# First expert job drawn from 13 tiles with its transposes behind the last logits; value sums in thirds; keys' first sums over all partitions

## The chip, the cores and the metric

The kernel runs on one NeuronCore of a Trainium2 chip. The metric is the device time of one execution in microseconds (us), the median of several runs; lower is better. The engines are TensorE (PE; its weight loads are listed as PEld), VectorE (DVE), ScalarE (ACT), GpSimd (POOL) and SyncE (SP, which here only issues DMAs). Each engine works through its own list of instructions in order; semaphores hold an instruction until what it reads is there and what it overwrites has been read. The lists are made ahead of time by a scheduler that moves instructions among each other by its own estimates; only dependencies and a few hand-written constraints bind it.

## The reference

Four batches of 8 heads with 576 positions of 64 values go through an attention that adds two parts: a full softmax attention over sums of four neighbouring positions, repeated four times, and a local one over positions less than 4 apart. The result, 2304 tokens of 512, goes through two mixture-of-experts layers, each with 8 experts.

```python
q_d = q.reshape(B, H, Sd, 4, D).mean(axis=3)           # k_d, v_d alike
out_up = np.repeat(sm_attn(q_d, k_d, v_d), 4, axis=2)
...
mask = np.abs(pos[:, None] - pos[None, :]) < 4
...
attn_out = out_up + np.matmul(attn, v)
x = attn_out.transpose(0, 2, 1, 3).reshape(B * S, H * D)
...
e_idx = np.argmax(x @ w_gate, axis=1)                   # one expert for each token
for e in range(8):
    h = np.maximum(x[e_idx == e] @ w1[e], 0.0)          # 512 -> 1024
    out[e_idx == e] = gate * (h @ w2[e])                # 1024 -> 512
```

The first layer has a second gate on its output. With these inputs the first layer sends 404 of the 2304 tokens to expert 0, the most, and 361 to expert 3. Of the first 14 tiles (1616 tokens) expert 0 has 253 and expert 3 has 244; of the first 13 tiles (1500 tokens) they have 242 and 236.

## The kernel before

**Attention.** `attention()` walks over 20 tiles (`NTP` = 5 for each batch) of up to 116 tokens in a software pipeline: in step `s` tile `s` has its local scores (`Local.scores`, L606) and softmax, tile `s-1` its transposes and products (L663), and tile `s-2` is turned (`xflip`, L683, `xtevac`, L687) and multiplied with the gate weights (`lmm`, L377, then `lsel`, L702, and a copy to `lgs`, L705). The pooled attention of a batch (`Pooled`) runs in the steps of the batch before; batch 0's runs ahead of the loop, in an order written by hand (`PRO`).

**The pooled sums.** `sums_k` adds four keys at a time into `kpd`, `sums_q` queries into `qd`, `sums_v` values into `vpd`. DVE does batch 0 (keys and queries with a reduction, L465) and POOL nearly all else (two additions: a first level into `tm`, L467, a second from it, L468; for the values L471 within `vraw`, then L474). Keys of the two heads of a pair lie in the lower and upper 64 partitions and go to different places of `kpd`, so `sums_k` runs once for each half of the partitions.

**Routing.** Tiles are routed in groups (`GROUPS`, first tile and count). When a group's last tile has its logits, `pick` finds each token's expert, `count` (matmuls L286 to L293 into `pos`) numbers the tokens within each expert, `place` (L309 to L337) computes each token's place and adds the group's totals to `base` (L311), and for each tile `spread` (L344 to L350: `am`, `oc`, `bm`) and `put` (a matmul into the PSUM tile `list`, L357) write token number and gate into the expert's list. `lT` (logits) and `pos` share one PSUM buffer, `ps_misc`. From step `PUTS` on two puts are issued in a step.

**The first expert job.** At the end of step `SNAP` `early()` runs: `snap` takes the expert that has the most tokens in the groups that are placed by then, `fetch` reads its first 256 entries from the list (`li`, L1039; `ri`, L1161) and POOL gathers those rows of `x0` (two indirect DMAs, L1144). `seen` tells which rows of `x0` that gather can touch. If the expert has fewer than 256 tokens so far, the rest of the job is empty rows, and its later tokens start at place 256. `prime` starts the loads of the first three weight tiles (`raw`). Behind attention `xpose` turns the gathered rows (L1194), ACT makes `xh` (L1198) and DVE the remainder `xl` (L1201); `split_next` does the same to weights (`wh`, L1115; `wl`, L1123). The first `wh` is held behind tile 19's L687 by a hand-written constraint.

**The jobs.** A product is three matmuls (`mm3`, L1276 to L1278). Job 0 is 192 such matmuls of 256 columns, `ph` then `py`, and the last groups' puts stand among them. Job 1 takes the same expert's remaining tokens from the finished lists and reuses its weights; a loop for experts whose lists overflow their job (`overflow`, L1284) follows, with no passes if every list fits. Seven more jobs with fixed sizes (`CAPS`) follow, and then the second layer.

Of the kernel before, what the change touches and what calls it, by code (L numbers as in the profile page):

```python
# [9 lines left out]
F32 = mybir.dt.float32  # L10
# [4 lines left out]
ALU = mybir.AluOpType  # L15
# [5 lines left out]
B, H, S, D = 4, 8, 576, 64  # L21
NP = H // 2
SD = S // 4
# [19 lines left out]
)  # L43

HEAD = (256, 256)
GROUPS = ((0, 5), (5, 4), (9, 5), (14, 4), (18, 2))
SNAP = 18
NWE = 3
POOLSPLIT = 0
POOLHI = 0  # L50
REM0 = 0
PUTN = 2
PB = (3, 2, 3, 2, 1)
PUTS = 15
PRI = 100
LOH = 1
NWARM = 3
# [123 lines left out]
def moe_pair_kernel(  # L181
# [17 lines left out]
    nc = tc.nc  # L199
# [164 lines left out]
    def route_all(*a, fast=0, **kw):  # L364
# [6 lines left out]
        for t in range(T):  # L371
            spread(t, fast)
            put(t)

    def logits(m, xT, n, lT, after=None):
        for g in range(4):
            i = nc.tensor.matmul(  # L377
                lT[32 * g:32 * g + 32, 0:n], lhsT=wgs[m][:, g, :], rhs=xT[:, g, 0:n],
                tile_position=(0, 32 * g), start=True, stop=True, skip_group_check=True,
            )  # L380
            if after is not None:
                tc.add_manual_dep(
                    i.ins, after.ins.name,
                    mybir.DependencyInfo(mybir.DependencyClass.Sync, mybir.DependencyReason.DATA),
                    reason="the four column tiles run side by side",
                )


    def attention(actx, early, early_x, front):
# [3 lines left out]
        sb2 = actx.enter_context(tc.tile_pool(name="a_sb2", bufs=2, side="right"))  # L393
# [5 lines left out]
        kd, qt = kq  # L399
        vd = [side[i].tile([128, NG, NP, D], F32, name=f"vd{i}") for i in range(2)]  # L400
        kpd = [side[i].tile([128, 2, NP, SD], F32, name=f"kpd{i}") for i in range(2)]
        vraw = sbe.tile([128, 3, 4, NP, 65], F32, name="vraw")
        vpd = [side[i].tile([128, 3, 2, NP, 65], F32, name=f"vpd{i}") for i in range(2)]
# [38 lines left out]
        def sums_k(b, c, n, eng=None):  # L442
            eng = eng or nc.vector
            a = slice(c, c + n)
            tm = tmp() if eng is nc.gpsimd else None
            for s in range(2):
                o = slice(64 * s, 64 * s + 64)
                src = kd[b % 3][o, a, 3:3 + S].rearrange("p a (t r) -> p a t r", r=4)
                pool4(eng, kpd[b % 2][o, s, a], src, tm[o, 0:n] if tm else None)

        def sums_q(b, c, n, eng=None):
            eng = eng or nc.vector
# [7 lines left out]
        def tmp():  # L460
            return sbe.tile([128, 2, SD, 2], F32, tag="tm", name="tm", bufs=2)

        def pool4(eng, dst, src, tm):
            if tm is None:
                eng.tensor_reduce(dst, src, axis=AX.X, op=ALU.add)  # L465
                return
            eng.tensor_tensor(tm, src[:, :, :, 0:2], src[:, :, :, 2:4], op=ALU.add)  # L467
            eng.tensor_tensor(dst, tm[:, :, :, 0], tm[:, :, :, 1], op=ALU.add)  # L468

        def sums_v(b, eng=nc.gpsimd):  # L470
            eng.tensor_tensor(vraw[:, :, 0:2], vraw[:, :, 0:2], vraw[:, :, 2:4], op=ALU.add)  # L471
            for s in range(2):
                o = 64 * s
                eng.tensor_tensor(  # L474
                    vpd[b % 2][o:o + 64, :, s], vraw[o:o + 64, :, 0], vraw[o:o + 64, :, 1], op=ALU.add
                )

        def sums(b, eng_q=None):
            for c in (0, 2):
# [230 lines left out]
        for b in range(B):  # L710
            s0 = NTP * (b - 1) + 2
            for c in range(NP + 1):
                if b or c == NP:
                    pooled_at.setdefault(s0 + c // 2 if b else REM0, []).append(Pooled(b, c))
        groups = GROUPS
        lgs_of = {}
# [29 lines left out]
        for i in range(3):  # L746
            t = sb3.tile([128, 3, 128], F32, tag="p", name="p")
# [58 lines left out]
        for s in range(-1, NL + 3):  # L806
# [6 lines left out]
            if 0 <= s:  # L813
                b, r = s // NTP + 1, s % NTP
# [9 lines left out]
            def ready1():  # L824
                for _ in range(PUTN if s > PUTS else 1):
                    if ready:
                        ready.pop(0)()

            def puts1():
                for _ in range(PUTN if s > PUTS else 1):  # L830
                    if puts:
# [78 lines left out]
            if 6 <= s < 12:  # L910
                o = 384 * (s - 6)
                tc.keep_in_program_order(
                    nc.sync.dma_start(x1[o:o + 384].rearrange("(k p) d -> p k d", p=128), bc1(zx, 3))
                )
            if s > SNAP:
                early_x(s)
            if s == SNAP:
                assert not (puts or defer)
# [39 lines left out]
    def experts():  # L958
# [195 lines left out]
        def fetch(job, fresh=None):  # L1154
# [7 lines left out]
            else:  # L1162
                nc.gpsimd.tensor_copy(ri[:, 0:ns], M.li[:, bass.ds(off, ns), :])
            tiles = max(g + n for g, n in GROUPS if g + n + 2 <= SNAP)
            seen = tiles // NTP * S + tiles % NTP * 2 * GQ
# [19 lines left out]
        def xpose(job, k):  # L1185
            if k == 0:
                xp = pl[f"x{job.i % 2}"]
                job.xT = tuple(xp.tile([128, 4, 512], F32R, tag=t, name=t) for t in ("xh", "xl"))
            xh, xl = job.xT
            mm = job.slots[k][1]  # L1190
            xr = job.x[k]
            pt = psx.tile([128, 4, 128], F32, tag="m", name="t")
            for d in range(4):
                nc.tensor.transpose(  # L1194
                    pt[:, d, 0:mm], xr[0:mm, 128 * d:128 * d + 128], ident[0:mm, 0:mm]
                )
            o = slice(128 * k, 128 * k + mm)
            i = nc.scalar.copy(xh[:, :, o], pt[:, :, 0:mm])  # L1198
            if job.i == 0:
                after.append(i)  # L1200
            nc.vector.tensor_tensor(xl[:, :, o], pt[:, :, 0:mm], xh[:, :, o].bitcast(F32), op=ALU.subtract)  # L1201
# [414 lines left out]
```

## Time and profile before

| | |
|---|---|
| median of 3 runs | 759.45 us (757.87 to 759.95) |
| the profiled execution's own time | 755.45 us |
| its span, first to last instruction | 753.7 us |
| PE busy | 700.1 us, 93% |
| DVE, ACT, POOL busy | 460.0, 342.4, 173.5 us |
| mean granted clock of PE | 0.967 of full speed |

All times below come from the profiled execution, counted from the start of its span. A matmul's busy time is modelled and the matmuls overlap, so a stretch that is fully busy is not a stretch at PE's peak. An instruction that is held inside its engine (not by a semaphore) is shown with a longer duration. The granted clock has two levels, 1.00 for 2.4 GHz and 0.50 for 1.2 GHz.

### The profile page before, as it was taken

The page shows a single profiled execution, that of the slowest core. Times are in us where ns is not written, and L with a number is a line of the kernel's source. Part 1 is how long each engine was busy: PE and PEld are TensorE (multiplying, and loading weights), DVE is VectorE, ACT ScalarE, POOL GpSimd, SP SyncE. Part 2 cuts the span into 40 slices and gives each one's busy share as a digit, 9 for nine tenths or more (in the row PEclk, how much of TensorE's full clock was granted, in tenths as well). Part 3 has the DMA queues.
Part 4 walks back from the last instruction along what each step waited for, and adds up shares of the span by engine and source line. Part 5 has one row for each costly group of instructions (what it writes and reads, how often), then busy time and mean ns, then how long its engine had stood idle before and what let it go on. Part 6 is the DMA issues. An engine that isn't in the chain of part 4 may idle for free. (4 is left out here: it accounts for less than half of the span.)

```text
span 753.7 us, 15825 instructions
## 1 busy us (share of the span) xinstructions
PE 700.1 (93%) x6048; PEld 642.4 (85%) x6048; DVE 460.0 (61%) x1169; ACT 342.4 (45%) x630; POOL 173.5 (23%) x202
## 2 busy tenths in 40 slices
PE   6788699995989999999999999989999999999993
PEld 4557477874979999999999999978999999999992
DVE  8787968786847656565757777535434444455520
ACT  2244366574444435345454463235425353554530
POOL 5774800001031203031211120152013030311111
PEclk9899989996999999999999999989999999999997
DMA  9935635135167535364555452256443544655500
GB/s 359 407 117 205 213 116 186 49 119 169 34 217 220 166 120 171 128 201 134 164 193 167 165 179 97 93 187 214 137 137 130 158 159 155 196 173 192 161 21 16
DMA packets 52990, 120.99 MB, mean 161 GB/s; under 512 B 4800, under 2 KB 26176, under 8 KB 51884
## 3 DMA queue, kind: packets, MB, share of 16 engines
q1 hardware_dynamic: 45772, 99.19, 39.6%
q0 software_dynamic: 7136, 20.72, 8.0%
q8 instruction: 50, 0.82, 0.4%
q14 instruction: 32, 0.26, 0.1%
HBM read 101.01 MB, written 20.71 MB: 162 GB/s over the span
## 5 line engine op out<-in xcount | busy, mean ns | idle before, releaser
L1123 DVE TENSOR_TENSOR wl<-raw,wh 128x1024 fp32r<-128x1024 f32 x128 | 156.2, 1224 | 111.2 <-ACT wh L1115 111.1
L1115 ACT CAST wh<-raw 128x1024 fp32r<-128x1024 f32 x128 | 133.1, 1048 | 199.1 <-PE py L1277 114.3
L1277 PE MATMUL ph<-xl,wh 128*128 128x256 f32 (+8 forms) x576 | 178.1, 311 | 0.2 <-DVE xl L1201 0.2
L1276 PE MATMUL ph<-xh,wh 128*128 128x256 f32 (+8 forms) x576 | 175.0, 312 | 2.6 <-DVE xl L1201 1.9
L1278 PE MATMUL ph<-xh,wl 128*128 128x256 f32 (+8 forms) x576 | 177.2, 309 | 0.0
L1276 PE MATMUL py<-h,wh 128*128 128x256 f32 (+8 forms) x448 | 138.5, 316 | 0.0
L1277 PE MATMUL py<-h,wh 128*128 128x256 f32 (+8 forms) x448 | 137.8, 311 | 0.0
L1278 PE MATMUL py<-h,wl 128*128 128x256 f32 (+8 forms) x448 | 137.3, 309 | 0.0
L1276 PEld LDWEIGHTS ph<-xh,wh 128*128 128x128 f32 x576 | 110.6, 195 | 4.8 <-DVE xl L1201 2.0
L1277 PEld LDWEIGHTS ph<-xl,wh 128*128 128x128 f32 x576 | 111.5, 194 | 1.1 <-DVE xl L1201 0.5
L1278 PEld LDWEIGHTS ph<-xh,wl 128*128 128x128 f32 x576 | 111.5, 194 | 0.6
L1403 DVE SCALAR_TENSOR_TENSOR h<-ph,h 128x256 fp32r<-128x256 f32 (+8 forms) x144 | 66.3, 471 | 40.9 <-ACT h L1402 40.4
L1402 ACT ACTIVATE h<-ph 128x256 fp32r<-128x256 f32 (+8 forms) x144 | 60.8, 423 | 55.9 <-PE ph L1278 54.7
L1277 PEld LDWEIGHTS py<-h,wh 128*128 128x128 f32 x448 | 84.2, 188 | 0.6
L1278 PEld LDWEIGHTS py<-h,wl 128*128 128x128 f32 x448 | 84.1, 188 | 0.6
L1276 PEld LDWEIGHTS py<-h,wh 128*128 128x128 f32 x448 | 83.5, 188 | 0.8
L1144 POOL DMA_INDIRECT xr<-x,ri x49 | 49.9, 1019 | 102.3 <-PE t L1194 79.4
L1204 POOL DMA_INDIRECT out<-yr,ri x25 | 25.8, 1031 | 128.9 <-ACT yr L1222 84.6
L1204 POOL DMA_INDIRECT x<-yr,ri x24 | 24.4, 1016 | 126.5 <-ACT yr L1222 118.0
L1476 DVE COPY yT<-py 128x256 f32<-128x256 f32 (+8 forms) x28 | 13.7, 489 | 39.9 <-PE py L1278 39.9
L1201 DVE TENSOR_TENSOR xl<-t,xh 128x512 fp32r<-128x512 f32 (+5 forms) x49 | 30.1, 620 | 12.2 <-ACT xh L1198 12.0
L1194 PE MATMUL t<-ident,xr 128*128 128x128 f32 (+5 forms) x196 | 29.6, 272 | 8.5 <-DMA xr<-x,ri 8.5
(193 smaller groups left out, 1037.3 us busy)
## 6 DMA issues: line engine op xcount, KB each, us to landing
raw<-w_a SPq DMA_DIRECT2D x64, 512.0 KB
raw<-w_b SPq DMA_DIRECT2D x64, 512.0 KB
vraw<-vr SPq DMA_DIRECT2D x4, 1560.0 KB
vd<-vw SPq DMA_DIRECT2D x4, 1280.0 KB
kd<-kT SPq DMA_DIRECT2D x8, 586.0 KB
qt<-qT SPq DMA_DIRECT2D x8, 586.0 KB
x<-zx SPq DMA_DIRECT2D x6, 768.0 KB
x<-x SPq DMA_DIRECT2D x36, 116.0 KB
```

Source lines behind the costliest of these rows:

```text
L1115: i = nc.scalar.copy(hi, raw)
L1123: i = nc.vector.tensor_tensor(lo, raw, hi.bitcast(F32), op=ALU.subtract)
L1144: g = nc.gpsimd.indirect_dma_start(xr[0:mm], None, src, bass.IndirectOffsetOnAxis(ap=ri[0:mm, k, 0:1], axis=0))
L1194: nc.tensor.transpose(pt[:, d, 0:mm], xr[0:mm, 128 * d:128 * d + 128], ident[0:mm, 0:mm])
L1201: nc.vector.tensor_tensor(xl[:, :, o], pt[:, :, 0:mm], xh[:, :, o].bitcast(F32), op=ALU.subtract)
L1204: i = nc.gpsimd.indirect_dma_start(M.dst[:, :], bass.IndirectOffsetOnAxis(ap=ri[0:mm, k, 1:2], axis=0), yr[0:mm], None, bounds_check=NT - ...
L1276: nc.tensor.matmul(ps, lhsT=ah, rhs=bh, start=first, stop=False)
L1277: nc.tensor.matmul(ps, lhsT=ah, rhs=bl, start=False, stop=False)
L1278: nc.tensor.matmul(ps, lhsT=al, rhs=bh, start=False, stop=last)
L1402: nc.scalar.activation(a[:, 0:n], ph[:, 0:n], func=AF.Relu)
L1403: nc.vector.scalar_tensor_tensor(b_[:, 0:n], ph[:, 0:n], 0.0, a[:, 0:n].bitcast(F32), op0=ALU.max, op1=ALU.subtract)
L1476: nc.vector.tensor_copy(yT[:, dc, 0:n], py[:, 0:n])
```

## The change

Four edits. The groups become (0,5), (5,4), (9,4), (13,5), (18,2), `SNAP` 17 and `PUTS` 13: the first job is drawn from 13 tiles, one step earlier, and tile 13 joins the group behind it. The transposes of job 0 must stand on PE behind the last logits matmul that was issued (`last`); this sets an order, not a wait. `sums_v` runs in thirds: three first-level additions of 128x520 and six of 64x260 in place of one of 128x1560 and two of 64x780, on POOL for batches 1 to 3 and on DVE for batch 0. `sums_k` does its first level over all 128 partitions: on POOL one addition instead of two, on DVE one reduction into a new tile `ks` that ACT copies in two halves into `kpd`.

```diff
-GROUPS = ((0, 5), (5, 4), (9, 5), (14, 4), (18, 2))
-SNAP = 18
+GROUPS = ((0, 5), (5, 4), (9, 4), (13, 5), (18, 2))
+SNAP = 17
...
-PUTS = 15
+PUTS = 13
...
+    last = [None]
...
                 tile_position=(0, 32 * g), start=True, stop=True, skip_group_check=True,
             )
+            last[0] = i
...
         def sums_k(b, c, n, eng=None):
             eng = eng or nc.vector
             a = slice(c, c + n)
-            tm = tmp() if eng is nc.gpsimd else None
+            src = kd[b % 3][:, a, 3:3 + S].rearrange("p a (t r) -> p a t r", r=4)
+            if eng is nc.vector:
+                tm = sb2.tile([128, 2, SD], F32, tag="ks", name="ks", bufs=1)[:, 0:n]
+                pool4(eng, tm, src, None)
+            else:
+                tm = tmp()[:, 0:n]
+                eng.tensor_tensor(tm, src[:, :, :, 0:2], src[:, :, :, 2:4], op=ALU.add)
             for s in range(2):
                 o = slice(64 * s, 64 * s + 64)
-                src = kd[b % 3][o, a, 3:3 + S].rearrange("p a (t r) -> p a t r", r=4)
-                pool4(eng, kpd[b % 2][o, s, a], src, tm[o, 0:n] if tm else None)
+                if eng is nc.vector:
+                    nc.scalar.copy(kpd[b % 2][o, s, a], tm[o])
+                else:
+                    eng.tensor_tensor(kpd[b % 2][o, s, a], tm[o, :, :, 0], tm[o, :, :, 1], op=ALU.add)
...
-            eng.tensor_tensor(vraw[:, :, 0:2], vraw[:, :, 0:2], vraw[:, :, 2:4], op=ALU.add)
-            for s in range(2):
-                o = 64 * s
-                eng.tensor_tensor(
-                    vpd[b % 2][o:o + 64, :, s], vraw[o:o + 64, :, 0], vraw[o:o + 64, :, 1], op=ALU.add
-                )
+            for k in range(3):
+                eng.tensor_tensor(vraw[:, k, 0:2], vraw[:, k, 0:2], vraw[:, k, 2:4], op=ALU.add)
+                for s in range(2):
+                    o = slice(64 * s, 64 * s + 64)
+                    eng.tensor_tensor(vpd[b % 2][o, k, s], vraw[o, k, 0], vraw[o, k, 1], op=ALU.add)
...
             for d in range(4):
-                nc.tensor.transpose(
+                i = nc.tensor.transpose(
                     pt[:, d, 0:mm], xr[0:mm, 128 * d:128 * d + 128], ident[0:mm, 0:mm]
                 )
+                if job.i == 0:
+                    tc.add_manual_dep(
+                        i.ins, last[0].ins.name,
+                        mybir.DependencyInfo(mybir.DependencyClass.NoSync, mybir.DependencyReason.DATA),
+                        reason="the last tokens' logits go ahead",
+                    )
```

The change moves line numbers (L1194 of before is L1204 of the change, L377 is L379, L465 is L476, L524 is L534, L1123 is L1133). Past the end of job 0 all engines have the same instructions in the same order. Three places differ in a way that the prediction speaks of.

The first place is PE between attention and job 0, before: `t<-ident,x` turns tile 19, `lT<-xT,wg` are its logits, `t<-ident,xr` are job 0's transposes, `pos` the counts of the group that ends with tile 17.

```order
L702 MATMUL lT<-cs,lts 128x16
L1194 MATMUL t<-ident,xr 128x128 x4
L286 LDWEIGHTS cb
L286 MATMUL pos<-ohb,cb 128x32
```

```order
L293 MATMUL pos<-ohb,cb 128x8
L1194 MATMUL t<-ident,xr 128x128 x4
L377 MATMUL lT<-xT,wg_79 32x128 x4
L1276 MATMUL ph<-xh,wh 128x256 x4
L702 MATMUL lT<-cs,lts 128x16
```

The same place of the change, from the counts' last rows on; the counts start right behind tile 18's L712.

```order
L712 MATMUL lT<-cs,lts 128x16
L286 LDWEIGHTS cb
L286 MATMUL pos<-ohb,cb 128x40
```

```order
L293 MATMUL pos<-ohb,cb 128x8
L379 MATMUL lT<-xT,wg_79 32x128 x4
L1204 MATMUL t<-ident,xr 128x128 x8
L712 MATMUL lT<-cs,lts 128x16
L1292 MATMUL ph<-xh,wh 128x256 x5
```

All eight transposes now stand behind the counts and behind the last logits. The puts for the first job moved as well: on PE the last of them stood 7 rows ahead of job 0's first transpose and now stands 54 rows ahead of it.

The second place is DVE in the start-up, before: `pmx` and `pd` are maxima and differences of batch 0's pooled scores, `mx` and `p` those of local tiles.

```order
L524 TENSOR_TENSOR pd_113<-s,pmx 128x2x3x48
L614 TENSOR_REDUCE mx<-s 128x8
L471 TENSOR_TENSOR vraw<-vraw 128x3x520
L521 TENSOR_REDUCE pmx<-s 128x2
L618 TENSOR_TENSOR p<-s,mx 128x2x4x64
L521 TENSOR_REDUCE pmx<-s 128x2
L614 TENSOR_REDUCE mx<-s 128x8
L474 TENSOR_TENSOR vpd_110<-vraw 64x3x260 x2
L524 TENSOR_TENSOR pd_114<-s,pmx 128x2x3x48
L524 TENSOR_TENSOR pd_115<-s,pmx 128x2x3x48
```

And DVE's list of the change.

```order
L534 TENSOR_TENSOR pd_114<-s,pmx 128x2x3x48
L483 TENSOR_TENSOR vraw<-vraw 128x520 x3
L531 TENSOR_REDUCE pmx<-s 128x2
L628 TENSOR_TENSOR p<-s,mx 128x2x4x64
L486 TENSOR_TENSOR vpd_110<-vraw 64x260 x2
L624 TENSOR_REDUCE mx<-s 128x8
L486 TENSOR_TENSOR vpd_110<-vraw 64x260 x4
L534 TENSOR_TENSOR pd_115<-s,pmx 128x2x3x48
```

One difference moved ahead of the value sums; the other stays behind them, and the sums of the second level are six instructions with one reduction among them.

The third place is DVE at the end of job 0, before: `bm` are the last group's spreads, `li` is the first copy of the finished lists, `yT` the copy of job 0's first output block.

```order
L350 TENSOR_TENSOR bm<-oc,v_2849 128x288 x2
L1403 SCALAR_TENSOR_TENSOR h_3122<-ph,h_3122 128x256
```

```order
L1060 TENSOR_TENSOR ov<-nr,cs 128x144
L1039 TENSOR_SCALAR li<-list_305 128x144
L1043 COPY lf<-list_305 128x144
```

And of the change.

```order
L350 TENSOR_TENSOR bm<-oc,v_2871 128x288
L1419 SCALAR_TENSOR_TENSOR h_3144<-ph,h_3144 128x256
L1133 TENSOR_TENSOR wl<-raw,wh 128x1024
```

```order
L344 TENSOR_SCALAR am<-cs,pp 128x128
L350 TENSOR_TENSOR bm<-oc,v_2871 128x288
```

```order
L1492 COPY yT<-py 128x256
L1049 TENSOR_SCALAR li<-list_319 128x144
```

The last spread moved behind one more weight tile, and `li` behind the first `yT`. Counted in PE's list, the last put stands behind 133 of job 0's 192 matmuls before and behind 155 now; there are seven puts in the job now, six before.

## Rows read from the trace of the kernel before

**Rows 1.** The page: busy tenths of PE in 40 equal slices of the span.

```profile
PE   6788699995989999999999999989999999999993
```

**Rows 2.** Stretches: length, busy time by engine, granted clock, DMA, GB/s.

```profile
220.00:700.00 480.00, 477.11 (x3316) 458.56 (x3316) 279.46 (x649) 221.77 (x363) 95.65 (x121) 0.99 0.51 164
175.00:189.00 14.00, 9.86 (x55) 8.64 (x56) 9.17 (x33) 5.11 (x9) 0.00 (x0) 0.51 0.53 175
48.00:54.00 6.00, 5.93 (x89) 4.44 (x90) 3.60 (x10) 3.54 (x9) 2.79 (x2) 0.72 0.49 161
88.00:96.00 8.00, 1.71 (x18) 0.85 (x16) 7.96 (x24) 1.23 (x4) 4.62 (x3) 0.82 0.37 139
93.00:101.00 8.00, 5.15 (x24) 4.63 (x24) 6.42 (x24) 5.97 (x18) 0.00 (x0) 0.57 0.39 125
```

**Rows 3.** The timeline before job 0: start, duration, instruction, idle ahead and releaser.

```profile
170.12 1.14 POOL L1144 DMA_INDIRECT xr<-x,ri  x1 [0.96 <-DMA raw<-w_a]
172.18 2.94 ACT L1115 CAST wh<-raw 128x1024 fp32r<-128x1024 f32 x3
177.02 1.09 PE L1194 MATMUL t<-ident,xr 128*128 128x128 f32 x4 [5.24 <-DMA xr<-x,ri]
178.99 1.22 DVE L1123 TENSOR_TENSOR wl<-raw,wh 128x1024 fp32r<-128x1024 f32 x1
182.53 0.68 DVE L1201 TENSOR_TENSOR xl<-t,xh 128x512 fp32r<-128x512 f32 x1
184.01 0.58 PE L1277 MATMUL ph<-xl,wh 128*128 128x256 f32 x1 [0.17 <-DVE xl L1201]
```

**Rows 4.** The timeline of PE at the end of job 0.

```profile
202.71 0.36 PE L357 MATMUL list<-bm,am 128*128 128x432 f32 x1
211.71 0.66 PE L1194 MATMUL t<-ident,xr 128*128 128x128 f32 x4 [1.03 <-DMA xr<-x,ri]
```

**Rows 5.** The groups of POOL, then DVE's reductions of keys: count, busy, mean ns.

```profile
L467 POOL TENSOR_TENSOR tm<-kd 64x576 f32<-64x576 f32 x12 | 14.6, 1212 | 16.7 <-DMA kd<-kT 11.6 <-DVE prd L574 4.4
L468 POOL TENSOR_TENSOR kpd<-tm 64x288 f32<-64x288 f32 x12 | 9.2, 767 | 1.1 <-POOL tm L467 0.5
L474 POOL TENSOR_TENSOR vpd<-vraw 64x780 f32<-64x780 f32 x6 | 11.5, 1909 | 0.3
L471 POOL TENSOR_TENSOR vraw<-vraw 128x1560 f32<-128x1560 f32 x3 | 10.5, 3499 | 11.2 <-DMA vraw<-vr 11.2
L465 DVE TENSOR_REDUCE kpd<-kd x4: 1346/1348/1351, 4.6 to 9.3; 64x288 f32<-64x1152 f32 x4
```

**Rows 6.** The timeline of the start-up.

```profile
16.68 2.98 POOL L467 TENSOR_TENSOR tm<-kd 64x576 f32<-64x576 f32 x2 [8.16 <-DMA kd<-kT]
17.66 2.83 DVE L474 TENSOR_TENSOR vpd<-vraw 64x780 f32<-64x780 f32 x2
21.08 2.41 PE L538 MATMUL t<-ident,pd 128*128 128x128 f32 x9 [5.77 <-issue]
28.34 0.42 DVE L577 TENSOR_TENSOR od<-v,prd 128x256 f32<-128x256 f32 x1
```

**Rows 7.** The timelines at the first stall; last, `od2l` with POOL still.

```profile
41.63 4.20 DVE L584 TENSOR_TENSOR od2l<-od,od2h 128x128 fp32r<-128x128 f32 x1
42.19 3.48 POOL L471 TENSOR_TENSOR vraw<-vraw 128x1560 f32<-128x1560 f32 x1
47.22 0.55 PE L538 MATMUL t<-ident,pd 128*128 128x128 f32 x3 [2.49 <-ACT pd L531]
L584 DVE TENSOR_TENSOR od2l<-od,od2h 128x128 fp32r<-128x128 f32 x2 | 0.6, 292 | 0.4 <-ACT od2h L583 0.3
```

**Rows 8.** DVE's timeline; PE's waits over attention: total, times, longest.

```profile
86.09 2.88 DVE L327 SCALAR_TENSOR_TENSOR den<-den,ez 128x5 f32<-128x5 f32 x1
PE lT L377 <- DVE gh L334: 2.7, 1, 2.7
PE list L357 <- ACT bm L348: 3.6, 1, 3.6
```

## The prediction

> **What bounds the kernel now.** I began with the page's row of PE's busy tenths [rows 1]: nines and eights nearly everywhere, with weak slices only in the first quarter (attention) and around slice 10 (the passage to the first job). The table by stretches [rows 2] says it harder. From 220 to 700 us PE is busy for 477.11 of 480.00 us at a granted clock of 0.99. Nothing in this change touches that stretch, and all engines have the same instruction order there, so whatever is won or lost before job 0 ends is handed on whole, and nothing can be won later. Three stretches ahead of it are not full, and I read those.
>
> The passage to job 0 [rows 2]: from 175 to 189 PE is busy 9.86 of 14 us, at clock 0.51. The timeline [rows 3] shows the chain. POOL's gather starts at 170.12, and PE then waits 5.24 us for its rows before the first transpose at 177.02. Since job 0's transposes stand in PE's list ahead of the last group's counts and of tile 19's logits, all that waits too. DVE makes the first weight remainder `wl` at 178.99, which on its own terms could have begun when the first `wh` was done (172.18 + 2.94/3 = 173.2), then two more, then `xl` at 182.53; the matmul that needs `xl` follows at 184.01.
>
> The end of job 0 [rows 4]: the last put runs at 202.71, and from it through the list, `li` and the next gather to job 1's transposes at 211.71 it takes 9.0 us, of which only 1.03 us is a wait of PE. This chain is just covered, so it may become the next limit.
>
> The rest is attention, where POOL's sums matter by their length.
>
> **The change, part by part.**
>
> *What POOL's instructions cost DVE.* The groups [rows 5] give 64x576 key additions at 1212 ns, second levels at 767, value sums at 1909 and 3499. They are off the critical path by themselves. But at the first stall [rows 7] DVE's `od2l`, two SBUF inputs, lasts 4.20 us while POOL runs the 3.48 us `vraw`, and it ends when that does; two others with POOL still take 292 ns. Likewise L327 at 86.09 [rows 8] lasts 2.88 us. So a DVE instruction of this kind is held for a whole POOL instruction, and shorter POOL instructions mean shorter holds. The Trainium skill (SBUF — State Buffer, "SBUF: two separate sides") says the same: the port pair that the two share is locked for the full instruction, and the loser blocks completely. By that rule alone the third that replaces 3.48 us holds `od2l` for about a third of it; the trace agrees for the whole one.
>
> Cutting could cost POOL a fixed part for each piece. Its rows give 1212/576 = 2.10 ns an element for the short first level and 3499/1560 = 2.24 for the long one, 767/288 = 2.66 and 1909/780 = 2.45 for the second levels [rows 5]: at most 0.2 ns on 288 elements, 60 ns, could be a fixed part. Nine pieces for three cost six times that, under 0.4 us per batch, on an engine with slack. The rule that speaks against the thirds is in the Trainium skill (GPSIMD Engine Reference, "Performance versus the Vector engine"): each GpSimd instruction goes through two software dispatch hops and a join of eight cores. It states no size for them; the rows leave those 60 ns, so I let nothing hang on it. Keys' first level over all partitions saves POOL one 1212 ns addition in each of six calls, 7.3 us, none of it on the path except where it shortens holds.
>
> 1. *Start-up: +2.3 (−0.7 to +4.2).* DVE does batch 0's value sums, before as two 780-element sums that took 2.83 us, held by POOL's key sums, which start at 16.68 [rows 6]; DVE was through at 20.49, and PE's transposes of `pd` came at 21.08. They were one for one with POOL: two instructions of POOL went by. Now six thirds stand there. If each again lets one POOL instruction by, six of POOL's (2 x 1.21 + 4 x 0.77 = 5.5 us) and six of DVE's (about 0.42 each, by the 256-element `od` [rows 6], 2.5 us) run end to end from 16.7 to 24.7: +4.2. Without holds it is 2.5 instead of 2.83, and one `pd`, about as long as `od`, is out of the way: −0.7. Two of the four reductions of 1.35 us [rows 5] leave DVE; its copies go to ACT, which is idle there; DVE then comes to the value sums about a microsecond earlier, with less of POOL beside it. I take a little over the middle, +2.3, since holding is what the rows show. It is handed on through `pd_115`, PE's transposes and `od` (28.34) [rows 6], which have no slack that I see.
>
> 2. *First stall: −3.2 (−4.2 to 0).* `od2l` waits for the running `kpd` and one third of `vraw` (3.48/3 = 1.2 us) rather than all: about 2.4 us earlier. PE's wait behind it is 2.49 at 47.22 [rows 7]; that goes. From 48 to 54 the clock is 0.72 [rows 2]: 6 x (1 − 0.72) = 1.7 us lost with PE 5.93 busy. It was low after that idle time; I count half of it as regained: 2.4 + 0.8 = 3.2. Everything gives 4.2; if POOL's thirds are let by in a row, 0.
>
> 3. *Second stall: −2.5 (−8.5 to 0).* PE works only 1.71 of 8 us from 88 to 96 [rows 2], in waits of 2.7 for `gh` and 3.6 for `bm` [rows 8], both ends of DVE's placing chain, in which L327, L310 and L336 were each held by one of POOL's three value sums. The clock is 0.57 from 93 to 101 [rows 2], about 2.2 us more with PE 5.15 busy (5.15 x 0.43). All of it: 8.5. But POOL's value work of batch 2 stays 3.5 + 2 x 1.9 = 7.3 us, and the chain has dozens of small instructions with two SBUF inputs, so nine pieces can catch nine of them. L327's hold falls from 2.88 to at most 1.2 and the later ones from at most 1.91 to 0.64, but there are more of them: I take about 2.5 off the first wait and leave the second.
>
> 4. *The passage: −5.3 (−6.9 to −2.6).* The snapshot is one step earlier; there are 20 tiles and two steps more ahead of the gather's 170.12, by estimate 7.7 us a step, so the rows land before tile 19 is through, and nothing on PE waits for them: the 5.24 goes. `wl` can start behind the first `wh`, at 173.4 instead of 178.99, and 3 x 1.22 later, at 177.1, `xl` follows instead of at 182.53 [rows 3]: 5.4 earlier, and the stream, tied to `xl`, 5.3. If the clock (0.51 from 175 to 189 [rows 2]) comes up sooner as well, I let it be 6.9, a third of what half clock takes from those 9.86 us busy; if DVE, with the tail of attention ahead of its `wl`, comes to them only half as much sooner, 2.6.
>
> 5. *Job 0's end: +0.5 (0 to +3.2).* The last put stands behind 155 instead of 133 of 192 matmuls. In the full stretch a matmul takes 480/3316 = 0.145 us on average [rows 2], so by that estimate 22 x 0.145 = 3.2 us of cover is lost from a chain that already waited 1.03 [rows 4]. The seventh put brings DVE about 0.8 us. Against that, the last group's counts start earlier by what PE no longer waits, so its spreads are ready sooner; as places in the list move by more than they do in time, I book 0.5.
>
> On SP the picked expert's value load and three weight loads now stand ahead of eight stores of `x0` rather than four; the weights come earlier, the stores later by four issues, and the gather waits only for rows of the first 13 tiles. I book nothing, and the price if I am wrong is a wait like the 5.24 back again.
>
> Sum: 2.3 − 3.2 − 2.5 − 5.3 + 0.5 = −8.2. The profiled execution took 755.45 us itself and would take 747.2; the runs' median is 759.45, and on that basis the forecast is **751.2**.
>
> **The rivals.** *Attention nets nothing* (start-up eats what the stalls give back): −5.3 + 0.5 gives 754.7. For it: POOL's total work is the same and DVE's holds are many. Against: the two stalls are each one long hold in front of PE.
>
> *Thirds are worth nothing and start-up pays in full*, as POOL lets its pieces by one after the other: +4.2 − 4.8 = −0.6, 758.9. `od2l` speaks for it, since it sat through the end of one POOL instruction and then all of the next.
>
> *Slower, by a full overflow pass.* The pick is made from 13 tiles. If it fell on an expert that hasn't the most tokens in the end, the jobs' fixed sizes would no longer fit the others, and a pass of the overflow loop would load two weight matrices, 4.2 MB, at 175 GB/s [rows 2] 24 us, of which perhaps 10 hide: 759.45 − 8.2 + 14 = 765. It decides as soon as one list is longer than its job. Against it: of 13 tiles expert 0 has 242 tokens and expert 3 has 236, so the pick stays. It is a margin of 6, but the data are fixed.
>
> *The first job doesn't start earlier*, because tile 19's own chain binds: then only attention's −3.4 remains: 756.1.
>
> **How the numbers follow.** The forecast has 0.55, attention at nothing 0.2, no earlier job 0 0.06, thirds worth nothing 0.13, the pass 0.03, and 0.03 is for other losses in start-up. 0.3%, some 2.3 us (757.2 to 761.7), is what can be told from no change. Faster takes the first two, most of the third: 0.79; same 0.14; slower 0.07. The forecast's own range, with the second stall between 0 and −5, is 747 to 754.5. From the bottom, both stalls whole would give +2.3 − 4.2 − 8.5 − 4.8 = −15.2, 744.3, and I leave out the last piece of that: 745.5. Upwards it takes in attention at nothing and ends between the last two cases, 757.5.
>
> **What would show it.** Right: no wait for gathered rows at job 0's first transpose; counts directly behind tile 18's logits; the first `wl` at about 173 less what attention gave; `od2l` under 2 us at the first stall, and no 2.49 wait of PE; a clock nearer 1 in 48 to 54; waits for `gh` below 1. Wrong: DVE's last value sum at 24.7 and `od` at 32 rather than about 30.6 in start-up; DVE instructions held as often as before beside the thirds; a wait of several microseconds at job 1's transposes for the second gather, which would show that the lists have become the limit; passes of the overflow loop.

## The result and the profile after

The changed kernel takes 748.16 us (median of 4 runs, 746.88 to 748.75) against 758.89 for the kernel before beside it (757.87 to 759.95): ratio 0.9863, 95% interval 0.9837 to 0.9889, or 10.7 us less by the medians (8 to 12 by the interval). The forecast was 751.2, 8.2 less. The profiled execution took 746.88 itself, span 745.1; that is 8.6 less than the profiled one of before, which was a quick one of its kind. Ratios leave out executions counted as slow, of which there was one (run 5, 759.54), while medians keep it.

The page's row of PE, which answers to [rows 1], has lost most of its weak slices in the first quarter (slices 3 to 5 were 8, 8 and 6, slice 10 was 5):

```profile
PE   7699999988899999999999999989999999999993
```

The table by stretches of the changed kernel, which answers to [rows 2] (length, busy time of PE, PEld, DVE, ACT, POOL, granted clock, DMA, GB/s):

```profile
220.00:700.00 480.00, 477.27 (x3309) 458.57 (x3309) 277.50 (x630) 222.13 (x363) 99.09 (x121) 0.99 0.50 162
44.00:54.00 10.00, 9.61 (x181) 6.76 (x179) 7.66 (x15) 5.58 (x13) 9.66 (x11) 1.00 0.37 118
80.00:104.00 24.00, 21.94 (x300) 16.90 (x299) 19.78 (x66) 14.75 (x39) 11.97 (x14) 0.93 0.55 191
153.00:163.00 10.00, 8.95 (x80) 7.69 (x81) 4.58 (x14) 2.95 (x7) 2.42 (x4) 0.66 0.32 103
```

The kernel before had in the two middle ones:

```profile
44.00:54.00 10.00, 7.20 (x98) 5.37 (x99) 7.56 (x15) 4.13 (x10) 6.63 (x5) 0.83 0.35 117
80.00:104.00 24.00, 16.01 (x209) 12.33 (x209) 22.30 (x65) 11.73 (x34) 10.76 (x7) 0.86 0.52 181
```

Past 220 PE is as full as before. At the first stall PE is now busy for 9.61 of 10 us and at full clock, and at the second for 21.94 of 24 instead of 16.01. New is a stretch at 153 to 163 with the clock at 0.66.

For bookkeeping I take the selection of a tile's logits (the copy to `lT` from `lts`), which each kernel does once per tile on PE. Tiles 0, 5, 7 and 16 in the kernel before:

```profile
44.43 0.29 PE L702 MATMUL lT<-cs,lts 128*128 128x16 f32 x2
...
81.26 0.40 PE L702 MATMUL lT<-cs,lts 128*128 128x16 f32 x2
...
109.48 0.40 PE L702 MATMUL lT<-cs,lts 128*128 128x16 f32 x2
...
163.18 0.29 PE L702 MATMUL lT<-cs,lts 128*128 128x16 f32 x2
```

And in the changed one:

```profile
47.74 0.29 PE L712 MATMUL lT<-cs,lts 128*128 128x16 f32 x2
...
79.17 0.29 PE L712 MATMUL lT<-cs,lts 128*128 128x16 f32 x2
...
99.62 0.37 PE L712 MATMUL lT<-cs,lts 128*128 128x16 f32 x2
...
153.82 0.29 PE L712 MATMUL lT<-cs,lts 128*128 128x16 f32 x2
```

By tile 16, before anything of the earlier first job can act on PE, 9.4 us are won (12.7 from tile 0 to tile 16, less the 3.3 by which tile 0 comes later); at the second group of job 1's transposes (203.08 below, 211.71 in [rows 4]) 8.6, and that is the span's difference. So in this pair of traces all of the gain is attention's, and the passage and job 0 together gave nothing. I had put 3.4 on attention and 4.8 on the rest.

### The profile page after: what moved, and what is told of

Same layout as the page of the kernel before. It is cut to its first block, busy times and chain, and to the rows that moved or that the text cites. A ratio compares the mean times of both kernels' runs of the same rounds, so it can differ in the third digit from the quotient of the medians.

```text
span 745.1 us, 15849 instructions
## 1 busy us (share of the span) xinstructions
PE 705.4 (95%) x6048; PEld 643.1 (86%) x6048; DVE 450.4 (60%) x1174; ACT 343.8 (46%) x633; POOL 172.8 (23%) x214
## 5 line engine op out<-in xcount | busy, mean ns | idle before, releaser
L1133 DVE TENSOR_TENSOR wl<-raw,wh 128x1024 fp32r<-128x1024 f32 x128 | 156.3, 1224 | 113.7 <-ACT wh L1125 113.6
L1154 POOL DMA_INDIRECT xr<-x,ri x49 | 51.9, 1060 | 99.2 <-PE t L1204 78.7
L1214 ACT CAST xh<-t 128x512 fp32r<-128x512 f32 (+5 forms) x49 | 26.0, 533 | 21.5 <-PE t L1204 21.4
```

What stands on the lines that cost most here:

```text
L1133: i = nc.vector.tensor_tensor(lo, raw, hi.bitcast(F32), op=ALU.subtract)
L1154: g = nc.gpsimd.indirect_dma_start(xr[0:mm], None, src, bass.IndirectOffsetOnAxis(ap=ri[0:mm, k, 0:1], axis=0))
```

## Experiments

Each ratio is to the kernel before on the same chip, with its 95% interval. One caution on single traces: the kernel before and the run "groups alone" have the same instruction order on PE until far past tile 0, and still their profiled executions differ by 3.1 us at tile 0, since from 32 to 36 us the one was granted full clock and the other half. The stretch of before, then of the groups alone:

```profile
32.00:36.00 4.00, 4.00 (x56) 2.53 (x55) 1.34 (x3) 0.74 (x2) 3.44 (x4) 1.00 1.06 437
```

```profile
32.00:36.00 4.00, 4.00 (x15) 1.48 (x16) 1.07 (x4) 0.40 (x1) 0.67 (x1) 0.50 1.05 433
```

The traces differ at the far end too. From the second group of job 1's transposes to the end, where the work is the same, it takes 538.9 to 539.1 us in runs 4, 7 and 11 and 541.7 to 544.2 in all others. The stretch from 480 to 500 of run 1, then of run 11:

```profile
480.00:500.00 20.00, 17.24 (x111) 15.57 (x110) 8.32 (x18) 8.28 (x13) 11.40 (x16) 0.91 0.63 205
```

```profile
480.00:500.00 20.00, 17.53 (x125) 15.82 (x124) 9.26 (x16) 9.53 (x17) 8.88 (x15) 1.00 0.70 217
```

So below, traces are compared by the distances between tile 0 and those transposes, and verdicts go by the timed runs. "The stream" is job 0's first matmul with `xl`.

**1. Attention's edits alone.** The changed kernel with

```diff
-GROUPS = ((0, 5), (5, 4), (9, 4), (13, 5), (18, 2))
-SNAP = 17
+GROUPS = ((0, 5), (5, 4), (9, 5), (14, 4), (18, 2))
+SNAP = 18
-PUTS = 13
+PUTS = 15
```

> The changed kernel with the groups, SNAP and PUTS of before; thirds, keys' sums and the order of the transposes stay. Theory 1 (shorter holds): what was won by tile 16 of attention in the changed kernel, 9.4 us, is won here too and handed on whole, with the wait of some 5 us for the gathered rows still in place: 750 to 751, 8 to 9 below the kernel before. Rival (the earlier first job is what counts): attention's gain is mostly lost again in the wait before job 0, 754 to 756.

745.92 us, ratio 0.9862 (0.9822 to 0.9901): the whole gain without the new groups, and 4 us below what Theory 1 gave. The transposes' order is in this run too, and in its trace PE waits 2.74 us for the gathered rows, not some 5.

**2. Groups alone.** `sums_v` and `sums_k` as before; groups, `SNAP`, `PUTS` and the order of the transposes as changed.

> The changed kernel with the value sums and the keys' sums of before: only groups, SNAP, PUTS and the order of the transposes change. Theory 1: the stalls stay, the matmul stream of job 0 starts some 5 us earlier, and the end of job 0 takes back 2 to 3 by later lists: 755.5 to 757. Rival (earlier first job): 5 us or more are kept, under 754. Rival 2 (job 0's end is all that counts, as the lists finish no sooner): 758 to 759.

758.14 us, ratio 1.0019 (0.9996 to 1.0041). Nothing, as rival 2 had it, and less than Theory 1 said. In its trace the stream starts 18.8 us behind tile 16 (20.8 before), and from there to the second group of job 1's transposes it takes 29.8 (27.7 before): what the passage gives, the end of job 0 takes.

**3. Without thirds.** The changed kernel with `sums_v` as before.

> The changed kernel with whole value sums: keys' first level over all partitions, groups and transposes stay. Theory 1 (holds by the length of POOL's value sums): the stalls in attention are back and the time is 754 to 757; DVE's od2l is held again for 3 us or more. Rival (POOL has less to do by 7.3 us through the keys, and this is what shortens attention): 748 to 750.5.

751.67 us, ratio 0.9922 (0.9897 to 0.9948): between the two. `od2l` is not held for 3 us or more, though POOL's `vraw` is whole again; its row of four reads min, median, max:

```profile
L595 DVE TENSOR_TENSOR od2l<-od,od2h x4: 292/294/1289, 42.0 to 148.4; 128x128 fp32r<-128x128 f32 x4
```

That is against my theory of the first stall: it was the keys' sums that removed this hold.

**4. Batch 0's values whole.** The changed kernel with, in `sums_v`,

```diff
+            if eng is nc.vector:
+                eng.tensor_tensor(vraw[:, :, 0:2], vraw[:, :, 0:2], vraw[:, :, 2:4], op=ALU.add)
...
+                return
```

> The changed kernel with batch 0's value sums on DVE whole as before, POOL's in thirds. My start-up term (thirds in start-up cost 2.3): 745.5 to 746.5. Rival (in start-up the thirds pay, as PE's products with the first third of the values begin while the others are still summed, or cost nothing): 748 to 750.

747.09 us, ratio 0.9886 (0.9851 to 0.9922), between the two expectations; the interval overlaps with the changed kernel's: the thirds of batch 0 cost nothing in start-up that can be measured.

**5. Thirds alone**, on the kernel before (`sums_v` as changed).

> The kernel before with the value sums in thirds, nothing else. If thirds and keys' sums act each by itself, this gives the difference of the changed kernel to the one without thirds, about -4: 753 to 755.5. If the thirds only pay once POOL's list is shortened by the keys' sums: 756.5 to 758.5.

752.48 us, ratio 0.9911 (0.9885 to 0.9938), some 5.4 by the medians and 6.7 by the ratio, a little more than the first expectation. The second stall goes (tile 5 to tile 7 takes 20.0 us instead of 28.2), the first doesn't: DVE, then POOL, at that place:

```profile
46.26 4.47 DVE L583 TENSOR_TENSOR od2l<-od,od2h 128x128 fp32r<-128x128 f32 x1
```

```profile
45.74 1.11 POOL L468 TENSOR_TENSOR kpd<-tm 64x288 f32<-64x288 f32 x1
46.82 3.76 POOL L472 TENSOR_TENSOR vraw<-vraw 128x520 f32<-128x520 f32 x3
```

`od2l` stands through the rest of `kpd` and three thirds in a row, and ends with the last of them. Cutting did not let it by.

**6. Keys' sums alone**, on the kernel before (`sums_k` as changed).

> The kernel before with keys' first sums over all partitions, nothing else. The run without thirds was 6 faster than before and the one with the groups alone no faster, so that the keys' sums would be worth 6 by themselves: 751 to 753. My prediction had booked nothing for them but fewer holds: 756 to 758.5.

753.53 us, ratio 0.9930 (0.9901 to 0.9959): 4.4 by the medians, 5.3 by the ratio, just above the first expectation. With run 5 it adds up to 9.8 (medians) or 12.0 (ratios), about what run 1 has in one, 11.8 or 10.5.

**7. Keys' sums on POOL only**: run 1 with, in `sums_k`, the code of before for DVE.

```diff
+            if eng is nc.vector:
+                for s in range(2):
...
+                    pool4(eng, kpd[b % 2][o, s, a], src, None)
+                return
```

> The run with attention's edits only, with batch 0's keys on DVE summed as before (two reductions for each pair of heads, no copies on ACT), POOL's over all partitions. If the gain of the keys' sums is POOL's (7.3 us less that can hold DVE): 745 to 747. If it is the start-up's (two reductions of 1.35 less ahead of the value sums): 748 to 751.

748.12 us, ratio 0.9885 (0.9860 to 0.9911): just inside the second expectation, but the start-up's part can't be told from nothing here (the intervals of runs 1 and 7 overlap).

**8. Snapshot a step later**: the changed kernel with

```diff
-SNAP = 17
+SNAP = 18
```

> The changed kernel with SNAP 18: the groups stay, the first job is still drawn from 13 tiles, but its list is read and its rows gathered one step later. If the passage gives nothing because the reading of the list stands on DVE ahead of tile 18's softmax (PE then waits 0.8 us for p and runs at half clock for 6.6 us): stream no later, 744 to 746.5. If job 0's end takes back whatever the passage gives: 746 to 748.5. If the early snapshot was what gave something: over 749.

748.33 us, ratio 0.9875 (0.9851 to 0.9899): the same as the changed kernel, inside the second expectation. But the edit did not move the snapshot. The lists of PE, ACT, POOL and SP in its trace are those of the changed kernel, and on DVE three instructions of one tile's softmax stand a place or two later. The list is read at tile 18 here too, the gather starts 0.32 us ahead of tile 16's selection (at 154.42) as it does in the changed kernel, and PE has the same wait for `p` (POOL, then PE):

```profile
154.10 1.14 POOL L1154 DMA_INDIRECT xr<-x,ri  x1 [0.96 <-DMA raw<-w_a]
```

```profile
155.51 0.39 PE L657 MATMUL v<-odh,rep 128*128 128x256 f32 x1 [0.80 <-DVE p L628]
```

So what the early snapshot is worth by itself was not tested, and this is one more trace of nearly the same lists. It differs in the clock, 1.00 where the changed kernel has 0.66 (153 to 163, above):

```profile
154.00:164.00 10.00, 8.12 (x130) 6.92 (x131) 6.08 (x26) 4.83 (x11) 2.48 (x4) 1.00 0.29 98
```

From tile 16 to the stream it needs 16.4 us instead of 18.8, and from there to the second group of job 1's transposes 35.4 instead of 30.5.

**9. Four raw weight buffers**: the changed kernel with

```diff
-NRAW = 3
+NRAW = 4
...
-yr = pl["y"].tile([128, DM], F32, tag="yr", name="yr", bufs=4)
+yr = pl["y"].tile([128, DM], F32, tag="yr", name="yr", bufs=3)
```

> The changed kernel with four buffers for raw weights in place of three (for the room, yr has three buffers in place of four). Theory 2 (the earlier passage is lost because DVE's fourth wl waits for a weight whose load could only be issued when the first wl had freed its buffer, with the spreads of the five-tile group queued behind that wl): the fourth weight is there, the wait of the lists' matmuls for bm goes, the last put comes earlier against the stream, and 2 to 4 us are won: 743.5 to 746. Rival (the lists' chain from the last logits is long in any case, or the transposes' second gather binds): 747 to 749.

752.40 us, ratio 0.9926 (0.9904 to 0.9948): slower than the changed kernel, and Theory 2 has not won. The wait of ACT, 4.65 us for the fourth weight in the changed kernel,

```profile
175.16 1.04 ACT L1125 CAST wh<-raw 128x1024 fp32r<-128x1024 f32 x1 [4.65 <-DMA raw<-w_a]
```

has only moved to the fifth; and since the four casts now run while the last tile is still under way, PE waits there (ACT, then PE, with four buffers):

```profile
179.24 1.04 ACT L1125 CAST wh<-raw 128x1024 fp32r<-128x1024 f32 x1 [3.85 <-DMA raw<-w_a]
```

```profile
166.59 0.65 PE L693 MATMUL t<-ident,x 128*128 128x128 f32 x4 [2.26 <-ACT x L682]
...
172.21 0.66 PE L379 MATMUL lT<-xT,wg 128*32 128x128 f32 x8 [2.86 <-DVE base L311]
...
183.51 0.47 PE L357 MATMUL list<-bm,am 128*128 128x432 f32 x1 [1.35 <-ACT bm L348]
```

A weight is still waited for ahead of `bm`, so the run doesn't show what job 0's end would be without such a wait.

**10. Control**: the changed kernel with three buffers for `yr`, as in 9.

> Control for the run with four raw buffers: the changed kernel with three buffers for yr, nothing else. PE is full past job 0 and the outputs are scattered behind it: within 1 us of the changed kernel, 747 to 749.

749.50 us, ratio 0.9882 (0.9862 to 0.9902), half a us above the expectation: no difference from the changed kernel that can be measured, so that the loss of run 9 is the buffers'.

**11. Sixths**: run 1 with

```diff
-                eng.tensor_tensor(vraw[:, k, 0:2], vraw[:, k, 0:2], vraw[:, k, 2:4], op=ALU.add)
+                for h in range(2 if eng is nc.gpsimd else 0):
+                    eng.tensor_tensor(vraw[:, k, h], vraw[:, k, h], vraw[:, k, h + 2], op=ALU.add)
+                if eng is nc.vector:
+                    eng.tensor_tensor(vraw[:, k, 0:2], vraw[:, k, 0:2], vraw[:, k, 2:4], op=ALU.add)
```

> The run with attention's edits only, with each first-level third on POOL cut into two instructions of 128x260. Theory 1 (a hold lasts as long as POOL's instruction): the longest of POOL's value sums falls from 1.2 to 0.6 us, which is worth up to 1 us more: 744.5 to 746. If POOL's pieces pass one after the other, or its fixed part counts: 746 to 749.

742.62 us, ratio 0.9794 (0.9773 to 0.9815): below every other kernel of the study, by more than expected. It beats the kernel before by 2.1%, and its interval lies apart from that of run 1. Its second stall, by stretch and by waits of PE:

```profile
80.00:104.00 24.00, 21.90 (x356) 17.30 (x360) 20.70 (x69) 16.44 (x42) 13.12 (x17) 1.00 0.60 208
```

```profile
PE list L357 <- DVE am L344: 1.0, 1, 1.0
```

The changed kernel has clock 0.93 there and a wait of 1.7 in that place. But that doesn't explain the time. Run 4 has thirds and the changed kernel's lists there, and its clock is 1.00 with PE busy 22.47 of the 24 us. From tile 0 to tile 16 run 11 takes 107.9 us, run 1 106.7. The 5.0 us between their traces are 0.9 up to tile 0, 1.7 in the passage, 0.9 at job 0's end and 2.8 past it, less 1.2 from tile 0 to tile 16. Also, the lists differ by more than the pieces: in job 0 the puts stand elsewhere on PE. That run 11 is faster is measured; that shorter holds in attention make it so is not shown.

**12. Run 1 with four raw buffers.**

> The run with attention's edits only (groups, SNAP and PUTS of before), with four raw buffers and three for yr. Theory 2 says that there the fourth weight waits as well (3.8 us on ACT), but PE lost less to it, 0.8 us: 743.5 to 746. Rival (the weights' loads don't bind the old groups): the same as without, 745 to 747.5.

750.40 us, ratio 0.9893 (0.9848 to 0.9939), from runs that scatter between 745.78 and 756.16: no gain, if anything a loss.

## Why the time was forecast well and its reasons were not

The time came out near by luck, as two errors had opposite signs: attention's edits (with the transposes' order, run 1) were worth about 10.5 instead of 3.4, and the passage with job 0's end about nothing (run 2) instead of 4.8.

**The failed steps.** The first is the sentence on keys' sums, that they save 7.3 us, "none of it on the path except where it shortens holds". They are worth about as much as the thirds (runs 5 and 6, and 3 from the other side). The second is term 5, by which job 0's end takes back only 0.5 of what the passage gives; it took all of it. The third is the reason given for both stalls, shorter holds: what the traces show is that other instructions meet.

**Start-up, +2.3.** Mis-sized. DVE's six second levels are through at 22.45 (20.49 before, 24.7 if each let a POOL instruction by), and `od` starts at 28.81, 0.5 later than in [rows 6]:

```profile
17.03 1.71 DVE L486 TENSOR_TENSOR vpd<-vraw 64x260 f32<-64x260 f32 x2
18.77 0.69 DVE L624 TENSOR_REDUCE mx<-s 128x8 f32<-128x512 f32 x1
19.49 2.96 DVE L486 TENSOR_TENSOR vpd<-vraw 64x260 f32<-64x260 f32 x4
...
28.81 0.42 DVE L587 TENSOR_TENSOR od<-v,prd 128x256 f32<-128x256 f32 x1
```

Run 4 gives it no measurable cost. I had not seen that a third of the values is enough for PE's first products, which start at 18.88 in this trace and at 20.24 in run 4's with whole sums.

**First stall, −3.2.** The signs came: the wait of 2.49 is gone, the clock is 1.00, and `od2l` lasts 1.29. From tile 0 to tile 5 the time falls by 5.4, more than the term's bound of 4.2. At that place (DVE, then POOL):

```profile
43.83 1.29 DVE L594 TENSOR_TENSOR od2l<-od,od2h 128x128 fp32r<-128x128 f32 x1
```

```profile
43.44 1.53 POOL L478 TENSOR_TENSOR tm<-qt 128x576 f32<-128x576 f32 x1
44.94 3.83 POOL L483 TENSOR_TENSOR vraw<-vraw 128x520 f32<-128x520 f32 x3
```

The reason is wrong. What holds it here is the queries' `tm`, and it passes ahead of the three thirds. Run 5 has the thirds and not the pass (4.47 us), runs 3 and 6 the pass without thirds. The keys' sums take POOL through its list sooner, so that another pair meets; but between tiles 0 and 5 the time only falls with both edits (36.8 us before, 37.3 with thirds alone, 38.0 with keys alone, 31.4 with both). The whole sums of runs 3 and 6 hold another instruction instead, `odl` some 24 us later (run 6, DVE, then POOL; run 3 has the same 3.75):

```profile
65.58 3.75 DVE L592 TENSOR_TENSOR odl<-od,odh 128x256 fp32r<-128x256 f32 x1 [0.47 <-ACT odh L591]
```

```profile
65.53 3.51 POOL L479 TENSOR_TENSOR vraw<-vraw 128x1560 f32<-128x1560 f32 x1 [7.88 <-DMA vraw<-vr]
```

**Second stall, −2.5.** Tile 5 to tile 7 takes 20.5 us instead of 28.2, near the bound of 8.5, and the waits of 2.7 and 3.6 have become one of 1.7. The mechanism was another. I had let nine pieces catch nine instructions of the placing chain; now the chain and the sums no longer meet. Before, the value sums of batch 2 start just ahead of L327:

```profile
85.45 3.50 POOL L471 TENSOR_TENSOR vraw<-vraw 128x1560 f32<-128x1560 f32 x1 [1.68 <-DMA vraw<-vr]
```

In the changed kernel the chain is through L337 at 85.8, and those sums start behind it (DVE, then POOL):

```profile
83.47 0.16 DVE L327 SCALAR_TENSOR_TENSOR den<-den,ez 128x5 f32<-128x5 f32 x1
```

```profile
90.48 4.23 POOL L483 TENSOR_TENSOR vraw<-vraw 128x520 f32<-128x520 f32 x3 [7.35 <-PE s L616]
```

Thirds alone have it so as well (L337 at 90.66, sums from 95.84). In run 7 the sums start at 86.20, behind L337 at 84.79 but beside the spreads, and the stretch takes 25.8. With whole sums and the keys' edit (runs 3 and 6) the sums run ahead of the chain, and it takes 22.7 and 23.7. So what the thirds give here is for the most part a matter of when the sums run. Whole, thirds and sixths give 758, 748 and 743, but the last step can't be put down to this place (run 11).

**POOL's fixed part.** I read at most 60 ns from four lengths, which was too little even by those rows: 767 ns for 288 elements and 1909 for 780 lie on a line with 98 ns at no elements. The three lengths of the first level now give it better: 3484 ns for 1560 elements, 1282 for 520, 731 for 260 (shortest of each; before, the changed kernel, run 11) lie on 181 ns + 2.12 ns an element. The rule that I let nothing hang on (the Trainium skill, GPSIMD Engine Reference, "Performance versus the Vector engine") was the better reading, though nine pieces for three cost POOL only 1.1 us a batch, and the kernel with twelve is faster still.

**The passage, −5.3, and job 0's end, +0.5.** From tile 16 to the stream the changed kernel takes 18.8 us instead of 20.8, and from there to the second group of job 1's transposes 30.5 instead of 27.7: 2.0 won and 2.8 lost. The mechanics of the passage are as forecast: the gather is early, and nothing waits for it (POOL, then PE):

```profile
153.50 1.15 POOL L1154 DMA_INDIRECT xr<-x,ri  x1 [0.96 <-DMA raw<-w_a]
```

```profile
154.92 0.39 PE L657 MATMUL v<-odh,rep 128*128 128x256 f32 x1 [0.81 <-DVE p L628]
...
167.81 1.09 PE L1204 MATMUL t<-ident,xr 128*128 128x128 f32 x8
...
169.59 0.61 PE L712 MATMUL lT<-cs,lts 128*128 128x16 f32 x2 [0.69 <-ACT lts L705]
...
172.63 0.58 PE L1293 MATMUL ph<-xl,wh 128*128 128x256 f32 x1 [0.24 <-DVE xl L1217]
...
179.43 0.46 PE L357 MATMUL list<-bm,am 128*128 128x432 f32 x1 [0.97 <-ACT bm L348]
...
195.18 0.36 PE L357 MATMUL list<-bm,am 128*128 128x432 f32 x1
...
203.08 0.66 PE L1204 MATMUL t<-ident,xr 128*128 128x128 f32 x4 [1.16 <-DMA xr<-x,ri]
```

An earlier stream does not bring job 1 forward. The changed kernel and runs 4, 8 and 10 have the same lists past the start-up, but for up to four instructions of a softmax on DVE. From tile 16 to the stream they take 18.8, 16.1, 16.4 and 18.8 us, from there to the second group of job 1's transposes 30.5, 33.6, 35.4 and 30.9: 49.3, 49.7, 51.8 and 49.7 in sum, against 48.5 before. So with the clock at 1.00 in the tail of attention (runs 4 and 8) the passage did give 4.7 and 4.4 of the 5.3, and job 0's end took all of it.

The half clock from 156 to 163 in the changed kernel is not explained. The reading of the list (`li`, `lf`, `tb`, six instructions of DVE from 151.91 to 155.08, mixed into the softmax) stands at tile 18 there, and PE waits 0.81 for `p`; but runs 4 and 8 have that reading and a wait of 0.81 and 0.80 at a clock of 1.00.

At job 0's end it is the puts that come late. The selection of tile 19, whose logits are the last, is at 169.59 above; before it was here:

```profile
180.96 0.44 PE L702 MATMUL lT<-cs,lts 128*128 128x16 f32 x2
```

From it to the last put (195.18 above, 202.71 in [rows 4]) the seven kernels with the old groups take 20.9 to 22.4 us (before, runs 1, 5, 6, 7, 11 and 12), the seven with the new ones 24.1 to 30.8 (the changed kernel, runs 2, 3, 4, 8, 9 and 10). So the new groups, with `PUTS`, go with some 2 to 10 us more in the chain that ends in job 1's gather. I had that loss in view as 3.2 at worst, as cover lost behind 22 matmuls, and booked 0.5 "as places in the list move by more than they do in time"; but the chain doesn't start with the stream, so an earlier stream is not handed on.

Why the chain stretches is open. The traces point at the loads of the weights: the six kernels with new groups and three raw buffers start the fourth `wh` 20.9 to 21.8 us behind tile 16, however early the stream is. Where ACT waits 4.7 to 4.9 us for that weight (the changed kernel, runs 2 and 10), selection to last put takes 24.4 to 25.8 us; where it waits 6.7 to 7.4 (runs 3, 4 and 8), 29.1 to 30.8. ACT's `bm` for the first put stands behind that `wh` and two more in its list. Run 9 moved the wait rather than removing it, so it doesn't settle this.

That the transposes now stand behind the last logits may be a gain of its own: runs 1, 7 and 11 take 16.1 to 17.8 us from tile 16 to the stream and 44.4 to 46.9 to the second group of job 1's transposes with the old groups, before and runs 5 and 6, which lack that order, 20.8 to 21.7 and 48.5 to 49.5. Run 12, with the order and four raw buffers, takes 21.8 and 48.9. It was not run alone. If it is a gain, a part of run 1's 10.5 is due to it, and the new groups cost what it gives.

**Rivals.** "Thirds are worth nothing, as POOL lets its pieces by one after the other" fits the first stall of run 5; at the second, the pieces come too late to meet the chain. "The first job doesn't start earlier" (756.1) had the right outcome for the groups in time, for another reason. The forecast's own range was wider than its condition: with the second stall between 0 and −5 the sum gives 748.7 to 753.7, not 747 to 754.5. The overflow pass did not occur: each layer's weights are loaded in 64 pieces as before.

## What to carry to other kernels

When a stretch later on is full, ask of an earlier start what the next link in the chain is, and measure the chain to that link, not to the first instruction that starts sooner. Work that is "off the path" on an engine that blocks another by its instructions is not free: how much of it there is and when it runs shift which instructions meet. A sum that fits the measured time does not prove its terms; two runs with half of the change each would have shown that at once. And when an edit goes through a scheduler, see in the trace that it moved what it was meant to move, and nothing else: one constant here left the lists as they were (run 8), and cutting POOL's sums moved puts on PE (run 11).

## What the runs showed of the hardware that I had not expected

A DVE instruction with two inputs in SBUF can be held through a run of POOL instructions, not just one: `od2l` 4.47 us through the rest of `kpd` and three `vraw` of 1.25 us each. In other traces the same instruction got in behind one POOL instruction and ahead of such a run (1.29 us). The Trainium skill (SBUF — State Buffer, "SBUF: two separate sides") gives the pair to whichever starts first, for the whole instruction; these rows agree with the blocking, and do not fit a lock that the longer waiter gets as soon as one instruction ends. What decides it, no run here shows.

The same instruction order gave executions 3.1 us apart at tile 0, with the granted clock in start-up at 0.50 or 1.00 (32 to 36 us). In the tail of attention one order ran at 0.66 or at 1.00 (the changed kernel, run 8), and reached the stream 18.8 or 16.4 us behind tile 16. What sets the level in one execution and not in another, no run here shows.
